# Retention with two gated layers: where queries are decayed, who copies the outputs, and in which order scores are made

## The chip, the cores and the metric

The kernel runs on one core of a Trainium2 chip. The metric is the device time of one launch in microseconds (us), the median of several runs. The core has five engines that work side by side, each in the order of its own queue: TensorE (PE, with its weight loads as PEld), VectorE (DVE), ScalarE (ACT), GpSimd (POOL) and SyncE (SP), which here issues the DMAs.

## The reference, cut to what matters

```python
scores = q @ k^T / sqrt(64)                    # B=4, H=8, S=576, head size 64
Dmat   = gamma_h ** (i - j) for i >= j, else 0 # gamma_h = 1 - 2**(-5-h)
ret    = (scores * Dmat) @ v                   # retention, no softmax
x = ret as (2304, 512)
x = (h * tanh(softplus(h))) @ w_out,  h = x @ w_in      # first layer, "mish", 512 -> 2048 -> 512
out = (h * sigmoid(1.702 h)) @ w2_out, h = x @ w2_in    # second layer
```

## The kernel before, in words

**Retention.** A batch of 576 tokens is cut into five chunks, four of 128 tokens and a last one of 64; batch by batch they make 20 units, u = 0 to 19. The unit's tile `unit` (1 MB; `rest`, 512 KB, for the short ones, units 4, 9, 14 and 19) holds q and k transposed, and v and k by token. The decay gamma^(i-j) is split into a factor for the query, in the table `gt`, and one for the value, in `vt`, so that only a causal mask `cm` is left for the scores. Each unit takes these steps:

- `decay_v(u)`: POOL multiplies v by `vt` in place (line 866).
- `scores(u)`: PE makes k^T q for 8 heads (`sc`, line 875), DVE masks them into two tiles `pm` (line 879).
- `update(u)` and `take(u)`: PE adds k^T v to the running sums `ds` (line 898), ACT copies them to `state` (line 133, two instructions). Short units have neither.
- `outputs(u)`: PE adds the earlier state times q (line 926; not in the first unit of a batch) and v times `pm` (line 938) in a bank `o`.
- `finish(u)`: the rows of `o` are multiplied by `gt` and put into X (line 956, DVE).

The loop over u writes these out by hand; each engine follows the order in which they are written. In step u stand `decay_v(u + 1)`, then POOL's share of other jobs, then `scores(u + 1)`, `update(u)`, `take(u)`, `outputs(u)`, ACT's early jobs, `finish(u)`, DVE's jobs, ACT's late jobs, and in eight units a piece of `split_x` (ACT, then DVE line 403), which splits X into a high and a low part for the first layer.

**The other jobs** are the conversions of the first layer's weights, one of which starts every unit or so, in pieces that `position(name, step)` hands out: DVE clamps (line 202), ACT scales (line 133, two instructions), DVE masks and shifts (lines 142 and 214), POOL joins (line 218), ACT rounds to the high part, DVE subtracts to get the low part (line 250). Weights 0 start in units 8 and 9, weights 1 in units 13 and 14, weights 2 in unit 18.

**The layers.** The first product of the first layer (`up`, line 416) already starts in steps 17 and 18, between the last units; then PE goes through 32 slots of the first layer, and through the rest of the program.

The banks are fixed: scores rotate over banks 0 to 3 (two per unit), `o` over 6 and 7, `ds` over 4 and 5.

Of the kernel before, what the change touches and what calls it, by code (L numbers as in the profile page):

```python
# [8 lines left out]
F32 = mybir.dt.float32  # L9
# [4 lines left out]
AF = mybir.ActivationFunctionType  # L14
ALU = mybir.AluOpType
# [5 lines left out]
P = 128  # L21
NPAIR = H // 2
# [3 lines left out]
CH = [(c, min(P, S - c)) for c in range(0, S, P)]  # L26
NCH = len(CH)
UNITS = [(b, c) for b in range(B) for c in range(NCH)]
# [31 lines left out]
REST = CH[-1][1]  # L60
SPLIT = 5
LAST = 2 * NPAIR * REST + DM

# [35 lines left out]
def retention_mish_gelu_kernel(ctx: ExitStack, tc: tile.TileContext, qkv, w1, w2, first_unit, rests, out):  # L101
    nc = tc.nc
    keep = ctx.enter_context(tc.tile_pool(name="keep", bufs=1))
# [4 lines left out]
    def cut(k, o, n):  # L108

        s, o = divmod(o, 2 * TH)  # L110
        assert o + n <= 2 * TH
        return X[:, s, k, o : o + n]
# [12 lines left out]
    def bank(kind, of):  # L125
        taken[kind] = taken.get(kind, -1) + 1
        return ps.tile([P, NB], F32, tag=f"b{of[taken[kind] % len(of)]}", name=kind)

    def quarters(t):
        return t.rearrange("p (c n) -> p c n", c=NPAIR)  # L130

    def act(o, i, f=AF.Copy, scale=1.0, bias=0.0):
        nc.scalar.activation(out=o, in_=i, func=f, scale=scale, bias=bias)  # L133
# [22 lines left out]
    def position(name, step):  # L156
        for j in [j for j in under_way if j[1] == name]:
            j[1] = next(j[0], None)
            if j[1] is None:
                under_way.remove(j)  # L160
        while plans.get(name) and plans[name][0][0] <= step:
            job = plans[name].pop(0)[1]
            then = next(job, None)
            if then:
                under_way.append([job, then])
# [197 lines left out]
    n_u = len(UNITS)  # L363
# [22 lines left out]


    xs, hs, gs, acc, side = {}, {}, {}, {}, []

    column = keep.tile([P, 32], F32, name="column")  # L390

    def split_x(t, k):

# [402 lines left out]
    def attention():  # L796
        with tc.tile_pool(name="att", bufs=1) as ap:
            loaded = {}
# [10 lines left out]
            def load(u):  # L809

                b, c = UNITS[u]
                if c == NCH - 1:
                    t = ap.tile([P, LAST], F32, tag="rest", name="rest", bufs=2)
                    nc.sync.dma_start(out=t, in_=rests[b])
                    loaded[u] = views(t, REST)
                    return
                t = buffers[(u - b) % len(buffers)]
                if u == 0:
                    for e0, e in ((0, 2 * DM), (2 * DM, FIRST)):
                        nc.sync.dma_start(out=t[:, e0:e], in_=first_unit[:, e0:e])  # L820
                else:
                    for e in (0, 2 * DM) if u == 1 else (0,):
                        e1 = e + 2 * DM if u == 1 else 4 * DM
                        nc.sync.dma_start(out=t[:, e:e1], in_=qkv[b, c, :, e:e1])
                loaded[u] = views(t, P)

            state = [ap.tile([P, NPAIR, P], F32, name=f"state{i}") for i in range(2)]
# [17 lines left out]
                out=cm, in_=cm, pattern=[[1, P]], compare_op=ALU.is_ge, fill=0.0, base=0, channel_multiplier=-1  # L845
            )
            gt = ap.tile([P, NCH, NPAIR, P], F32, name="gt")
# [3 lines left out]
            for _ in range(WARM):  # L851
                nc.tensor.matmul(unused, lhsT=zeros, rhs=zeros, start=True, stop=True)

            act(column[:, :1], state[0][:, 0, :1], AF.Mish)

            for u in range(1, NCH + 1):
                load(u)
            pm, sums, now = {}, [None], [None]

            def decay_v(u):  # L860
                b, c = UNITS[u]
                n = CH[c][1]
                vv = loaded[u][2][:n].rearrange("p (h d) -> p h d", d=D)
                for eng, h, e in ((nc.vector, 0, SPLIT), (nc.gpsimd, SPLIT, H)) if u == 0 else ((nc.gpsimd, 0, H),):
                    by = vt[:n, c, h:e].unsqueeze(2).to_broadcast([n, e - h, D])
                    eng.tensor_tensor(out=vv[:, h:e], in0=vv[:, h:e], in1=by, op=ALU.mult)

            def scores(u):
                n = CH[UNITS[u][1]][1]
                qt, kt = loaded[u][:2]  # L870
                sc = [quarters(bank("sc", (0, 1, 2, 3))) for _ in range(2)]
                for p in range(NPAIR):
                    for j in range(2):
                        sl = slice(64 * j, 64 * j + 64)
                        nc.tensor.matmul(sc[j][:n, p, :n], lhsT=kt[sl, p, :], rhs=qt[sl, p, :], start=True, stop=True)  # L875
                pm[u] = []
                for j in range(2):
                    t = ap.tile([P, NPAIR, P], F32, tag="pm", name="pm", bufs=4)
                    nc.vector.tensor_tensor(
                        out=t[:n, :, :n],  # L880
                        in0=sc[j][:n, :, :n],
                        in1=cm[:n, :n].unsqueeze(1).to_broadcast([n, NPAIR, n]),
                        op=ALU.mult,
                    )
                    pm[u].append(t)

            def update(u):

                c = UNITS[u][1]
                if c == NCH - 1:  # L890
                    return
                v, kk = loaded[u][2:]
                if c == 0:
                    sums[0] = quarters(bank("ds", (4, 5)))
                for p in range(NPAIR):
                    for j in range(2):
                        sl = slice(p * P + 64 * j, p * P + 64 * j + 64)
                        nc.tensor.matmul(  # L898
                            sums[0][64 * j : 64 * j + 64, p, :D],
                            lhsT=kk[:, sl],  # L900
                            rhs=v[:, sl],
                            start=(c == 0 and p == 0),
                            stop=True,
                            skip_group_check=True,
                        )
# [43 lines left out]
            def finish(u, o):  # L949
                b, c = UNITS[u]  # L950
                t0, n = CH[c]
                g0 = b * S + t0
                part = 0
                while part < n:
                    w = min(n - part, 2 * TH - (g0 + part) % (2 * TH))
                    nc.vector.tensor_tensor(
                        out=cut(slice(None), g0 + part, w),
                        in0=o[:, :, part : part + w],
                        in1=gt[:, c, :, part : part + w],
                        op=ALU.mult,  # L960
                    )
                    part += w

            decay_v(0)
# [5 lines left out]
            for u in range(n_u):  # L970
                step = u - n_u
                if u - 1 in wide and wide.index(u - 1) + len(buffers) < len(wide):
                    n = wide[wide.index(u - 1) + len(buffers)]
                    load(n)
                    if n + 1 not in wide:
                        load(n + 1)
                if u + 1 < n_u:
                    decay_v(u + 1)
                position("pool", step)
                position("fetch", step)  # L980
                if u == 0:
                    for n in wide[NCH : len(buffers)]:
                        load(n)
                if NCH - 1 <= u < n_u - 1:
                    scores(u + 1)
                before = now[0]

                def step_state():
                    update(u)
                    now[0] = take(u)  # L990

                if u != 1:
                    step_state()
                o = outputs(u, before, *((step_state,) if u == 1 else ()))
                if 0 < u < NCH - 1:
                    scores(u + 1)
                if u < NCH - 1:
                    n = CH[u + 1][1]
                    for p in range(NPAIR):
                        act(gt[:, u + 1, p, :n], gt[:, 0, p, :n], scale=steps[:, p, u + 1 : u + 2])  # L1000
                position("act early", step)

                if u == n_u - 2:
                    elementwise(0, jobs=False)
                finish(u, o)
                if u == n_u - 1:
                    elementwise(1, jobs=False)
                if u == 0:
                    scores(1)
                position("vector", step)  # L1010
                position("act late", step)
                if u in X_UNITS:
                    k = X_UNITS.index(u)
                    split_x((0, SIDE)[k // NK], k % NK)()
                if u == n_u - 3:
                    up(0)
                if u == n_u - 2:
                    up(1)
# [266 lines left out]
```

## Time and profile before

| | before |
|---|---|
| median of 3 runs (lowest, highest) | 807.36 us (807.34, 808.15) |
| the profiled execution's own time | 807.84 us |
| its span, first to last instruction | 806.1 us |
| PE busy | 801.2 us (99%) |
| DVE, ACT, POOL busy | 571.2, 442.0, 189.3 us |
| mean granted TensorE clock | 0.999 |
| retention, from the first score to the last output | about 5 to 70 us |

The span is what the trace shows; the 1.7 us between it and the execution's time lie before the first and after the last instruction. A busy PE says only that a matmul was under way; whether it was held up is read from the distance of the starts in the timeline.

### The profile page before, as it was taken

Reading aid. Unit: us, or ns where it says so; the run is one execution under the profiler, and the core shown is the slowest. Engines: PE = TensorE matmul, PEld = TensorE weight load, DVE = VectorE, ACT = ScalarE, POOL = GpSimd, SP = SyncE. Lnnn points to the kernel's source line nnn. Section 1 sums busy time; section 2 is a strip of 40 time slices with the busy share of each in tenths; the row PEclk is TensorE's granted clock in tenths of the full one; section 3 lists DMA queues with packets and bytes.
Section 4 is the critical chain, followed back from the end, with each engine's and each line's share of the span. In section 5 each row is a group of like instructions: output and inputs, shape, how many; then the busy total and the mean of one; then the engine's idle time right before and its main releaser. Section 6 shows DMA issues by size and latency. Waiting matters only on the chain.

```text
span 806.1 us, 14287 instructions
## 1 busy us (share of the span) xinstructions
PE 801.2 (99%) x5394; PEld 761.7 (94%) x5394; DVE 571.2 (71%) x992; ACT 442.0 (55%) x861; POOL 189.3 (23%) x251
## 2 busy tenths in 40 slices
PE   9999999999999999999999999999999999999998
PEld 8998888889999999999999999999999999999998
DVE  3897988877687676567677376798555897656775
ACT  5355867765766565666566454665233663234542
POOL 3352322220376460366570052000000000000000
PEclk9999999999999999999999999999999999999999
DMA  9994679746799895698986599888887888878884
GB/s 363 420 375 123 231 235 287 273 143 214 275 309 327 297 336 177 204 324 310 341 289 219 200 351 382 272 275 270 291 255 253 252 272 291 272 253 257 251 272 158
DMA packets 92325, 219.68 MB, mean 273 GB/s; under 512 B 6496, under 2 KB 52576, under 8 KB 90464
## 3 DMA queue, kind: packets, MB, share of 16 engines
q1 hardware_dynamic: 92112, 218.56, 80.4%
q8 instruction: 43, 0.70, 0.3%
q14 instruction: 26, 0.21, 0.1%
q10 hardware_dynamic: 144, 0.20, 0.1%
HBM read 169.98 MB, written 48.76 MB: 271 GB/s over the span
## 4 chain that ended last, share of the span: by engine, by line
PE 97%; DVE 1%; DMA 1%; ACT 0%; POOL 0%; issue 0%; SPq 0%
PE p L731 22%; PE p L682 21%; PE acc L1093 17%; PE p L1156 15%; PE h L416 8%; PE acc L437 8%; PE sc L875 2%; PE o L938 2%; PE o L926 2%; PE ds L898 1%; DMA unit<-first_unit_dram 1%; DVE cs L475 0%; DVE u L475 0%; DVE X L142 0%; ACT cs L133 0%; DVE cy L352 0%
## 5 line engine op out<-in xcount | busy, mean ns | idle before, releaser
L682 PE MATMUL p<-xop,ring 128*128 128x384 f32 x1008 | 175.6, 334 | 0.4 <-DVE cs L475 0.4
L682 PEld LDWEIGHTS p<-xop,ring 128*128 128x128 f32 x1008 | 174.7, 188 | 0.8 <-DVE cs L475 0.7
L731 PE MATMUL p<-g,ring 128*128 128x384 f32 x1008 | 175.2, 334 | 0.0
L731 PEld LDWEIGHTS p<-g,ring 128*128 128x128 f32 x1008 | 174.8, 188 | 0.0
L1093 PE MATMUL acc<-g,w 128*128 128x512 f32 (+1 forms) x768 | 143.7, 337 | 0.0
L1093 PEld LDWEIGHTS acc<-g,w 128*128 128x128 f32 x768 | 124.3, 188 | 17.1 <-DVE g L475 0.2
L1156 PE MATMUL p<-xop,ring 128*128 128x384 f32 x672 | 128.4, 337 | 0.0
L1156 PEld LDWEIGHTS p<-xop,ring 128*128 128x128 f32 x672 | 115.7, 188 | 0.3
L133 ACT ACTIVATE g<-cs 128x384 fp32r<-128x384 f32 x168 | 79.0, 517 | 60.3 <-PE p L731 60.0
L475 DVE TENSOR_TENSOR g<-cs,g 128x384 fp32r<-128x384 f32 x168 | 90.0, 554 | 26.7 <-ACT g L133 25.0
L133 ACT ACTIVATE cs<-cs 128x384 f32<-128x384 f32 x72 | 37.8, 526 | 104.7 <-DVE cs L475 104.7
L437 PE MATMUL acc<-g,w 128*128 128x512 f32 (+1 forms) x384 | 72.3, 337 | 0.0
L475 DVE TENSOR_TENSOR g<-c,g 128x384 fp32r<-128x384 f32 x64 | 44.4, 693 | 38.9 <-ACT g L133 38.5
L437 PEld LDWEIGHTS acc<-g,w 128*128 128x128 f32 x384 | 60.2, 190 | 7.6
L133 ACT ACTIVATE c<-p 128x384 f32<-128x384 f32 x64 | 31.2, 488 | 52.7 <-PE p L1156 52.5
L218 POOL TENSOR_TENSOR raw<-raw 128x512 int32<-128x512 int32 x32 | 36.5, 1141 | 96.3 <-DVE raw L214 87.0
L342 POOL TENSOR_TENSOR cy<-cy 128x128 f32<-128x128 f32 x88 | 54.3, 626 | 5.2
L475 DVE TENSOR_TENSOR cs<-cs 128x384 f32<-128x384 f32 x96 | 53.4, 556 | 0.8
L416 PE MATMUL h<-x,w 128*128 128x512 f32 x192 | 46.4, 390 | 0.0
L218 POOL TENSOR_TENSOR cy<-cr 128x256 int32<-128x256 int32 x38 | 31.2, 842 | 62.7 <-DVE cr L214 58.3
L133 ACT ACTIVATE raw<-raw 128x512 int32<-128x512 uint32 x64 | 40.6, 679 | 7.8 <-DVE raw L202 7.5
L475 DVE TENSOR_TENSOR c<-p,c 128x384 f32<-128x384 f32 x48 | 26.5, 553 | 23.9 <-ACT c L133 12.9
(94 smaller groups left out, 971.6 us busy)
## 6 DMA issues: line engine op xcount, KB each, us to landing
ring<-stream SPq DMA_DIRECT2D x168, 512.0 KB, 4.6
ring<-first_stream SPq DMA_DIRECT2D x56, 512.0 KB, 5.5
stream<-cy SPq DMA_DIRECT2D x22, 896.0 KB, 5.0
raw<-w_dram SPq DMA_DIRECT2D x32, 512.0 KB, 8.0
unit<-qkv_dram SPq DMA_DIRECT2D x14, 1024.0 KB, 13.4
cr<-w_dram SPq DMA_DIRECT2D x19, 512.0 KB, 5.7
stream<-X SPq DMA_DIRECT2D x10, 896.0 KB, 5.4
first_stream<-cy SPq DMA_DIRECT2D x16, 512.0 KB, 3.0
```

What stands on the lines that cost most here:

```text
L133: nc.scalar.activation(out=o, in_=i, func=f, scale=scale, bias=bias)
L218: nc.gpsimd.tensor_tensor(out=o, in0=upper, in1=bits, op=ALU.add)
L342: nc.gpsimd.tensor_tensor(out=v[:, o], in0=v[:, a], in1=v[:, b], op=op)
L416: nc.tensor.matmul(h[:, :n], lhsT=W[0, m // 2][:, m % 2, a, k * P : (k + 1) * P], rhs=xs[t, k][:, b, :n], start=((k, a, b) == order[0]), s ...
L437: nc.tensor.matmul(acc[t, e][:, :n], lhsT=W[1, m // 2][:, m % 2, a, e * P : (e + 1) * P], rhs=g[:, b, :n],  start=(begins(i) and a == 0 an ...
L475: eng.tensor_tensor(out=o, in0=a, in1=b, op=op)
L682: nc.tensor.matmul(banks[p], lhsT=w[:, k, a * P : (a + 1) * P], rhs=x[:, b, k], start=(p not in SAME and k == 0 and a == 0 and b == 0), st ...
L731: nc.tensor.matmul(banks[e, p], lhsT=w[:, e, a * P : (a + 1) * P], rhs=g[:, b], start=(p != 2 and r == 0 and a == 0 and b == 0), stop=(r = ...
L875: nc.tensor.matmul(sc[j][:n, p, :n], lhsT=kt[sl, p, :], rhs=qt[sl, p, :], start=True, stop=True)
L926: nc.tensor.matmul(o[sl, p, :n], lhsT=before[:, p, sl], rhs=qt[:, p, :], start=(p == 0), stop=True, skip_group_check=True,)
L1093: nc.tensor.matmul(acc[t, e][:, :w], lhsT=W[1, m // 2][:, m % 2, a, e * P : (e + 1) * P], rhs=g[:, b, o : o + w], start=(m == 0 and a == 0 ...
L1156: nc.tensor.matmul(bank, lhsT=w[:, a, k * P : (k + 1) * P], rhs=x[:, b, k], start=(p in (1, 2, 7) and k == 0 and a == 0 and b == 0), stop= ...
```

## The change

From unit 6 on (`SCALED`), the decay of the query is applied to q instead of to the output: a new `decay_q(u)` on POOL multiplies the query part of the unit's tile by `gt` in place, two steps ahead (three for units 11 to 19) of the step in which the unit's outputs are made, and `finish(u)` is a plain copy on ACT. From unit 12 on (`TWICE`), the scores of two units are made one after the other in every second step. `pm` gets six buffers instead of four, and a scratch column is dropped (its one use writes into `gt`, ahead of the table).

```diff
+SCALED = 6
+TWICE = 12
...
-    column = keep.tile([P, 32], F32, name="column")
...
-            act(column[:, :1], state[0][:, 0, :1], AF.Mish)
+            act(gt[:, 0, 0, :1], state[0][:, 0, :1], AF.Mish)
...
+            def decay_q(u):
+                c = UNITS[u][1]
+                n = CH[c][1]
+                nc.gpsimd.tensor_tensor(out=loaded[u][0], in0=loaded[u][0], in1=gt[:, c, :, :n], op=ALU.mult)
...
-                    t = ap.tile([P, NPAIR, P], F32, tag="pm", name="pm", bufs=4)
+                    t = ap.tile([P, NPAIR, P], F32, tag="pm", name="pm", bufs=6)
...
-                    nc.vector.tensor_tensor(
-                        out=cut(slice(None), g0 + part, w),
-                        in0=o[:, :, part : part + w],
-                        in1=gt[:, c, :, part : part + w],
-                        op=ALU.mult,
-                    )
+                    to, of = cut(slice(None), g0 + part, w), o[:, :, part : part + w]
+                    if u >= SCALED:
+                        act(to, of)
+                    else:
+                        nc.vector.tensor_tensor(out=to, in0=of, in1=gt[:, c, :, part : part + w], op=ALU.mult)
...
+                for n in range(SCALED, n_u):
+                    if u == n - 2 - (n > TWICE - 2):
+                        decay_q(n)
                 position("pool", step)
...
-                    scores(u + 1)
+                    for n in (u + 1,) if u + 1 < TWICE else (u + 1, u + 2) if (u + 1 - TWICE) % 2 == 0 else ():
+                        scores(n)
```

**PE, from the scores of unit 12 to those of unit 15, before.** `sc` are scores, `ds` the sums, `o` the outputs (from `state`, then from `pm`).

```order
L875 MATMUL sc<-unit 128x128 x8
L898 MATMUL ds<-unit 64x64 x8
L926 MATMUL o<-unit,state_72 64x128 x8
L938 MATMUL o<-pm,unit 64x128 x8
L875 MATMUL sc<-unit 128x128 x8
L898 MATMUL ds<-unit 64x64 x8
L926 MATMUL o<-unit,state_73 64x128 x8
L938 MATMUL o<-pm,unit 64x128 x8
L875 MATMUL sc<-rest 64x64 x8
```

PE at the same place, from the scores of units 12 and 13 on, in the changed kernel (its lines are numbered a little higher: 880 is 875, 903 is 898, 931 is 926, 943 is 938):

```order
L880 MATMUL sc<-unit 128x128 x16
L903 MATMUL ds<-unit 64x64 x8
L931 MATMUL o<-unit,state_71 64x128 x8
L943 MATMUL o<-pm,unit 64x128 x8
L903 MATMUL ds<-unit 64x64 x8
L931 MATMUL o<-unit,state_72 64x128 x8
L943 MATMUL o<-pm,unit 64x128 x8
L880 MATMUL sc<-rest 64x64 x8
L880 MATMUL sc<-unit_75 128x128 x8
```

The scores of unit 13 moved up beside those of unit 12, ahead of the sums and outputs of unit 11; those of unit 15 stand right behind those of unit 14.

**POOL, from v of unit 11 to v of unit 15, before.** Line 866 is `decay_v`, line 218 a weight's join.

```order
L866 TENSOR_TENSOR unit<-unit,unit_76 128x512
L218 TENSOR_TENSOR raw<-raw 128x512
L866 TENSOR_TENSOR unit<-unit,unit_76 128x512
L218 TENSOR_TENSOR raw<-raw 128x512
L866 TENSOR_TENSOR unit<-unit,unit_76 128x512
L866 TENSOR_TENSOR rest<-rest,unit_76 64x512
L866 TENSOR_TENSOR unit_76<-unit_76 128x512
```

POOL at the same place in the changed kernel, from v of unit 11 on; line 871 is `decay_q`, here for units 13, 14, 15, 16 and 17, and line 220 the join:

```order
L866 TENSOR_TENSOR unit<-unit,unit_75 128x512
L871 TENSOR_TENSOR unit<-unit,gt 128x512
L220 TENSOR_TENSOR raw<-raw 128x512
L866 TENSOR_TENSOR unit<-unit,unit_75 128x512
L871 TENSOR_TENSOR rest<-rest,gt 128x256
L220 TENSOR_TENSOR raw<-raw 128x512
L866 TENSOR_TENSOR unit<-unit,unit_75 128x512
L871 TENSOR_TENSOR unit_75<-unit_75,gt 128x512
L866 TENSOR_TENSOR rest<-rest,unit_75 64x512
L871 TENSOR_TENSOR unit_76<-unit_76,gt 128x512
L866 TENSOR_TENSOR unit_75<-unit_75 128x512
L871 TENSOR_TENSOR unit_77<-unit_77,gt 128x512
```

Between two operations on v there is now one on q, and the one on q is that of a unit two further on.

**DVE in steps 10 to 13, before**: masks (line 879), outputs (line 956), the first layer's operands (line 403) and weights (lines 142, 214, 250).

```order
L142 SCALAR_TENSOR_TENSOR raw<-raw 128x512
L214 TENSOR_SCALAR raw<-raw 128x512
L403 TENSOR_TENSOR side<-X,side 128x256
L879 TENSOR_TENSOR pm<-sc,cm 128x512 x2
L956 TENSOR_TENSOR X<-o,gt 128x4x128
L250 TENSOR_TENSOR w_622<-raw,w_622 128x512
L403 TENSOR_TENSOR side<-X,side 128x256
L879 TENSOR_TENSOR pm<-sc,cm 128x512 x2
L956 TENSOR_TENSOR X<-o,gt 128x4x128
L250 TENSOR_TENSOR w_673<-raw,w_673 128x512
L403 TENSOR_TENSOR side<-X,side 128x256
L879 TENSOR_TENSOR pm<-sc,cm 64x4x64 x2
```

DVE at the same place in the changed kernel; line 144 is 142, 216 is 214, 252 is 250, 884 is 879:

```order
L144 SCALAR_TENSOR_TENSOR raw<-raw 128x512
L216 TENSOR_SCALAR raw<-raw 128x512
L403 TENSOR_TENSOR side<-X,side 128x256
L884 TENSOR_TENSOR pm<-sc,cm 128x512 x4
L252 TENSOR_TENSOR w_629<-raw,w_629 128x512
L403 TENSOR_TENSOR side<-X,side 128x256
L252 TENSOR_TENSOR w_695<-raw,w_695 128x512
L403 TENSOR_TENSOR side<-X,side 128x256
L884 TENSOR_TENSOR pm<-sc,cm 64x4x64 x2
L884 TENSOR_TENSOR pm<-sc,cm 128x512 x2
```

The outputs are gone; the masks of units 12 and 13 stand together, and four operations on weights and operands stand in a row ahead of the mask of unit 14.

## Rows read from the trace of the kernel before

**Rows 1.** Page, chain that ended last: share of the span by engine

```profile
PE 97%; DVE 1%; DMA 1%; ACT 0%; POOL 0%; issue 0%; SPq 0%
```

**Rows 2.** Waits of PE, 0 to 170 us: us in total, times, longest

```profile
PE o L938 <- DVE pm L879: 0.2, 1, 0.2
```

**Rows 3.** Timeline of PE, units 11 to 15: start, duration, instructions

```profile
40.23 1.16 PE L875 MATMUL sc<-unit 64*128 64x128 f32 x16
41.33 0.69 PE L898 MATMUL ds<-unit 128*64 128x64 f32 x16
41.84 1.04 PE L926 MATMUL o<-unit,state 128*64 128x128 f32 x16
42.72 1.04 PE L938 MATMUL o<-pm,unit 128*64 128x128 f32 x16
43.69 1.16 PE L875 MATMUL sc<-unit 64*128 64x128 f32 x16
...
46.17 1.04 PE L938 MATMUL o<-pm,unit 128*64 128x128 f32 x16
47.15 0.68 PE L875 MATMUL sc<-rest 64*64 64x64 f32 x16
47.76 0.69 PE L898 MATMUL ds<-unit 128*64 128x64 f32 x16
...
51.83 0.68 PE L938 MATMUL o<-pm,rest 64*64 64x64 f32 x16
52.44 1.16 PE L875 MATMUL sc<-unit 64*128 64x128 f32 x16
53.53 0.69 PE L898 MATMUL ds<-unit 128*64 128x64 f32 x16
```

**Rows 4.** Groups by line and shape, 20 to 62 us: busy us, mean ns

```profile
L956 DVE TENSOR_TENSOR X<-o,gt 128x512 f32<-128x512 f32 x10 | 6.8, 682 | 1.5 <-PE o L938 1.5
L956 DVE TENSOR_TENSOR X<-o,gt 128x256 f32<-128x256 f32 x5 | 2.0, 414 | 0.9 <-PE o L938 0.9
L214 DVE TENSOR_SCALAR raw<-raw 128x512 int32<-128x512 int32 x4 | 1.7, 430 | 0.1
```

**Rows 5.** Groups of ACT by shape, 190 to 260 us

```profile
L133 ACT ACTIVATE X<-acc 128x512 f32<-128x512 f32 x2 | 1.2, 595 | 0.4 <-PE acc L437 0.4
```

**Rows 6.** Timeline of POOL, 32 to 48 us

```profile
32.85 1.04 POOL L866 TENSOR_TENSOR unit<-unit,unit 128x512 f32<-128x512 f32 x1 [3.98 <-DMA unit<-qkv_dram]
35.28 1.04 POOL L866 TENSOR_TENSOR unit<-unit,unit 128x512 f32<-128x512 f32 x1 [1.39 <-DMA unit<-qkv_dram]
...
43.98 1.04 POOL L866 TENSOR_TENSOR unit<-unit,unit 128x512 f32<-128x512 f32 x1
44.98 1.48 POOL L866 TENSOR_TENSOR rest<-rest,unit 64x512 f32<-64x512 f32 x1
46.43 1.04 POOL L866 TENSOR_TENSOR unit<-unit 128x512 f32<-128x512 f32 x1
```

**Rows 7.** Timeline of DVE, 44 to 51 us

```profile
44.83 0.73 DVE L250 TENSOR_TENSOR w<-raw,w 128x512 fp32r<-128x512 f32 x1
45.49 2.26 DVE L403 TENSOR_TENSOR side<-X,side 128x256 fp32r<-128x256 f32 x1
47.67 1.28 DVE L879 TENSOR_TENSOR pm<-sc,cm 128x512 f32<-128x512 f32 x2
...
50.35 0.41 DVE L403 TENSOR_TENSOR side<-X,side 128x256 fp32r<-128x256 f32 x1
50.69 0.74 DVE L879 TENSOR_TENSOR pm<-sc,cm 64x256 f32<-64x256 f32 x2
```

**Rows 8.** Timeline of ACT: the state of unit 15

```profile
54.32 0.78 ACT L133 ACTIVATE state<-ds 64x256 f32<-64x256 f32 x2 [1.25 <-PE ds L898]
```

**Rows 9.** Timeline of DVE: the low part of weights 2 of the first layer

```profile
77.16 0.68 DVE L250 TENSOR_TENSOR w<-raw,w 128x512 fp32r<-128x512 f32 x1
```

**Rows 10.** Timeline of PE: the product that takes weights 2

```profile
77.74 1.52 PE L416 MATMUL h<-x,w 128*128 128x512 f32 x6
```

## Prediction

> **What bounds it.** I first read the chain that ended last: PE holds 97% of the span [rows 1]. Then PE's waits over the retention and the first layer: a single one, of 0.2 us [rows 2]. So while the retention runs, PE is never kept waiting by the engines that the change relieves, and nothing taken from DVE or given to ACT or POOL is a gain by itself. What can be won is PE's own time, and for that the timeline's starts count, not its durations, since matmuls overlap. From one start to the next, the outputs from the state take 0.88 us (41.84 to 42.72), those from the masked scores 0.97 (42.72 to 43.69), the scores 1.09 (43.69 to 44.78), the sums 0.51 (41.33 to 41.84) [rows 3]. Outputs and scores are the same number of matmuls with the same 128 moving columns; what the scores have more, and what the outputs have more when scores follow, is the price of changing from tiles of 128 by 64 to 64 by 128 and back.
>
> **What the pairs save on PE.** Outputs before scores cost 0.97 - 0.88 = 0.09 more, scores 1.09 - 0.88 = 0.21 more, and sums behind scores 0.51 where half of 0.88, for half the columns, would be 0.44: 0.07 more. A round trip is thus 0.37 us with four places where it is paid, of which some belongs to the wider weights of the scores; I take 0.17 for one change of tiles. By the order, PE changes tiles 22 times from unit 12's scores to the first layer before, and 17 times after: the pairs 12 and 13, 16 and 17 save two changes each; 14 and 15, 18 and 19 pair a short unit's 64 by 64 tiles with a long one's and save less; the sums behind the product in step 17 cost one more kind of change and one less. Five times 0.17 is **-0.85 us**. Bounds: 0 (the extra belongs to the scores themselves) and -1.0.
>
> **What moves between the engines.** DVE loses ten wide and five narrow copies, 6.8 + 2.0 = 8.8 us [rows 4]. ACT gains them; the nearest row is its copy of 512 elements from a bank, 0.595 us [rows 5], so at most 15 x 0.6 = 9 us, hidden behind PE: a bank `o` is used again only two units on, some 3.5 us a unit later. POOL gains 14 multiplications. The nearest row is its multiplication of v at 1.04 us [rows 6]; for a short unit's 256 elements I take half, bounds 0.5 and 1.04. That is 11 x 1.04 + 3 x 0.5, some 13 us, in a stretch in which POOL sat idle for 1.4 to 4 us between units. For units 6 to 12 this idle time covers them. The dropped column and the two more buffers cost nothing: the write goes to the same engine that fills the table later, and the buffers remove a wait that PE does not have.
>
> **Where it does not fit.** In steps 10 to 14 POOL has 11 operations in a row (v and q of five units, two joins), and DVE has eight operations that touch POOL's port. What that costs stands in the rows: the weight subtraction at 44.83, 0.68 us alone [rows 9], found POOL busy from 43.98 to 45.02 and ended 0.54 us behind it; POOL's next multiplication then took 1.48 us where it takes 1.04, ending 0.90 us behind DVE's end. The narrow subtraction at 45.49, 0.41 us alone, took 2.26 us and ended at 47.75, 0.28 us behind the second of two POOL operations [rows 6, 7]. Masks read a bank, and keep their 0.64 us. So I let the two alternate: a DVE operation ends 0.28 us (narrow, clamp, shift) or 0.54 us (wide) after the POOL operation ahead of it, the next POOL operation 0.90 us after that. In the Trainium skill, SBUF — State Buffer, section "SBUF: two separate sides", DVE and POOL share a port pair as an exclusive lock, and whichever starts first holds it for its whole instruction. By that rule each wait lasts one operation, as in my sum; the row at 45.49 shows two, which is the rival below.
>
> Now the walk, in the clock of the rows before, against the times at which PE would come without waits.
> - Unit 13's q. Loads land 2.43 us apart (35.28 - 32.85 [rows 6], units 10 and 11, both waiting for them), so unit 13's lands near 40.1 (estimate). Then it takes its turn with a shift on DVE and ends near 41.3. PE wants it right behind unit 12's scores, at 40.23 + 0.99 = 41.22: **0.1 us**. (Before, at 43.69.)
> - Masks of unit 12. Ahead of them on DVE stand a clamp (ends 41.6), unit 11's masks (to 42.8), then line 142, which finds POOL at v of unit 12 (to 43.5; ends 44.05), the shift behind q of unit 14 (44.5; ends 44.8), and the narrow subtraction, which takes the port at once (45.15). Masks to 46.35. PE wants them at 46.17 - 0.34 = 45.83, with the wait above 45.95: **0.4 us**.
> - Unit 15's q. POOL goes on with the join (45.15 + 0.90 = 46.05), v of unit 13 (47.05), q of unit 15 (48.1). PE: unit 14's scores at 47.15 - 0.35, 0.61 for them, so 47.41, now 47.95: **0.1 us** more.
> - Masks of unit 14. Unit 13's are done at 47.55. Then two wide and two narrow subtractions, and POOL busy throughout with q 15, v 14, q 16, v 15: they end at 48.6, 49.8, 51.25 and 52.45, the mask (0.74 [rows 7]) at 53.1. PE wants it for `o` of unit 14 at 51.83 - 0.55 = 51.28, now 51.9: **1.1 us**. If nothing waited, the masks would be ready at 50.1; that is the lower bound, 0.
> - Unit 16's sums go into the bank from which ACT copies unit 15's state. That copy ended at 54.32 + 0.78 = 55.10 [rows 8], 1.57 us behind the start of the sums at 53.53. With no scores between, PE is there after 0.52 + 0.88 = 1.40: **0.2 us**.
>
> Behind these waits stand all of PE's later matmuls, since its queue is in order; nothing gives the time back, as PE is the chain. Later pairs have room: POOL's q 17 is ready a unit ahead. Sum: -0.85 + 0.1 + 0.4 + 0.1 + 1.1 + 0.2 = **+1.05 us**. The profiled execution took 807.84 us, 0.48 above the median, so against the median 807.36 this gives **808.4 us**.
>
> **The first layer** sets a cap on gains. The low part of weights 2 is ready at 77.16 + 0.68 = 77.84 [rows 9], and PE's product that needs it, from its third matmul on, begins at 77.74 [rows 10], some 0.45 us ahead of that matmul: 0.35 us to spare. DVE no longer has the last two outputs ahead of it, but ACT now waits there for unit 19's output before it can go on, so that chain comes perhaps 0.2 us earlier, not 0.85. A retention shorter by more than 0.55 us is not passed on in full. With the loss that I forecast this does not bind.
>
> **Rivals.**
> - The port costs little (DVE slips in between, or POOL is never so far behind): no more than the 0.1 and 0.2 us of the first and last item. The gain is then -0.85 + 0.3 = -0.55, just at the cap: 806.8 us. For it: the masks have 1.8 us of room if nothing waits, and DVE is 8.8 us lighter. Against: 11 POOL operations in a row, and rows 7.
> - DVE loses the port again and again, as at 45.49: each loss adds one POOL operation, 1.04 us, ahead of a mask that PE waits for. Two of them on the way to the masks of units 12 and 14 give 808.4 + 2.1 = 810.5 us. It is slower by over 0.2% from a sum of waits of 2.5 us on. For it: that row; against: in the same place DVE got the port after one operation.
> - The pairs save nothing, because the 0.21 us belongs to the scores' own wide weight loads: 807.36 + 1.9 = 809.3 us. For it: no row shows two wide scores in a row; against: the outputs ahead of the scores, with no wide weights, take 0.09 longer too.
>
> **How the numbers follow.** A change of 0.2%, 1.6 us, is about what a measurement of this kernel can tell from none. Forecast (807.7 to 809.0 us): 0.44. Cheap port (806.5 to 807.7): 0.27. Port lost repeatedly: 0.20. No saving: 0.05. Faster by more than 0.2% has no mechanism here, since PE's saving ends at 1.0 us; 0.04 is for what I overlook. Slower by over 0.2% is the third and fourth case and the edge of the first: 0.26; the same: 0.70. The range reaches from the cheap port's 806.6 us into the repeated losses, to 810.2.
>
> **What would show it.** After: the second scores of a pair follow the first after 1.0 us, not 1.09, and one pair saves 0.35 us. PE's waits should name POOL's q for the scores of units 13 and 15, DVE's masks for the outputs of units 12 and 14, and ACT's state for the sums of unit 16. DVE's subtractions at line 252 and 403 should take 1 us and more. I am wrong if PE still waits for nothing (then it is faster, by up to 0.55 us), or if waits come in units 6 to 11, which I took to be covered.

## The result: slower by 1.1%

The changed kernel took 816.56 us (median of 4 runs, 815.53 to 816.72) beside 807.64 us for the kernel before: a ratio of 1.0107, interval 1.0090 to 1.0125. The prediction of 808.4 us and its range up to 810.2 were wrong. Its profiled execution took 816.72 us with a span of 815.0 us, 8.9 us more than before; the mean clock was 0.996.

The chain that ended last, share of the span by engine, after, answers to [rows 1]:

```profile
PE 95%; DVE 3%; DMA 1%; issue 0%; ACT 0%; POOL 0%; SPq 0%
```

PE's share fell by two hundredths and DVE's rose by two. The waits of PE after (us in total, times, longest) say where; before, there was a single one of 0.2 us [rows 2], which is still there (at 7.56 us) as the shorter of the two for masks:

```profile
PE o L943 <- DVE pm L884: 4.7, 2, 4.5
PE sc L880 <- POOL unit L871: 1.0, 2, 0.8
```

The timeline of PE after (start, duration, instructions), from the scores of units 12 and 13 to the sums of unit 18, answers to [rows 3]:

```profile
40.14 1.16 PE L880 MATMUL sc<-unit 64*128 64x128 f32 x16
42.11 1.22 PE L880 MATMUL sc<-unit 64*128 64x128 f32 x16 [0.81 <-POOL unit L871]
43.26 0.69 PE L903 MATMUL ds<-unit 128*64 128x64 f32 x16
...
47.94 0.68 PE L880 MATMUL sc<-rest 64*64 64x64 f32 x16
48.85 1.16 PE L880 MATMUL sc<-unit 64*128 64x128 f32 x16 [0.23 <-POOL unit L871]
...
52.21 0.64 PE L931 MATMUL o<-rest,state 128*64 128x64 f32 x16
57.32 1.35 PE L943 MATMUL o<-pm,rest 64*64 64x64 f32 x16 [4.48 <-DVE pm L884]
58.61 3.78 PE L880 MATMUL sc<-unit 64*128 64x128 f32 x32
...
64.61 0.63 PE L903 MATMUL ds<-unit 128*64 128x64 f32 x16
...
73.95 0.69 PE L903 MATMUL ds<-unit 128*64 128x64 f32 x16
```

Two things are to be seen: the outputs of unit 14 from its masks come at 57.32, 5.1 us behind the outputs from the state; and behind them the scores of units 16 and 17 take 3.7 us until the next instruction, where the scores of two units otherwise take 2. What DVE and POOL did in those 5 us is in their timelines. Below, q 15 is short for POOL's multiplication of unit 15's queries (line 871), v 15 for that of its values (line 866). DVE, which answers to [rows 7]:

```profile
45.59 2.47 DVE L884 TENSOR_TENSOR pm<-sc,cm 128x512 f32<-128x512 f32 x4
47.98 1.36 DVE L252 TENSOR_TENSOR w<-raw,w 128x512 fp32r<-128x512 f32 x1
49.27 2.49 DVE L403 TENSOR_TENSOR side<-X,side 128x256 fp32r<-128x256 f32 x1
51.68 2.76 DVE L252 TENSOR_TENSOR w<-raw,w 128x512 fp32r<-128x512 f32 x1
54.37 2.48 DVE L403 TENSOR_TENSOR side<-X,side 128x256 fp32r<-128x256 f32 x1
56.77 1.93 DVE L884 TENSOR_TENSOR pm<-sc,cm 64x256 f32<-64x256 f32 x4
```

POOL, which answers to [rows 6]:

```profile
47.53 1.27 POOL L871 TENSOR_TENSOR unit<-unit,gt 128x512 f32<-128x512 f32 x1
48.76 1.49 POOL L866 TENSOR_TENSOR rest<-rest,unit 64x512 f32<-64x512 f32 x1
50.21 1.27 POOL L871 TENSOR_TENSOR unit<-unit,gt 128x512 f32<-128x512 f32 x1
51.44 1.22 POOL L866 TENSOR_TENSOR unit<-unit 128x512 f32<-128x512 f32 x1
52.63 1.27 POOL L871 TENSOR_TENSOR unit<-unit,gt 128x512 f32<-128x512 f32 x1
53.86 1.48 POOL L866 TENSOR_TENSOR unit<-unit,unit 128x512 f32<-128x512 f32 x1
55.31 1.25 POOL L871 TENSOR_TENSOR unit<-unit,gt 128x512 f32<-128x512 f32 x1
```

The four subtractions, 0.68 and 0.41 us alone, took 1.36, 2.49, 2.76 and 2.48. Lay their ends beside POOL's: the first ended at 49.34, 0.54 behind the multiplication of q 15 (48.80); the second at 51.76, 0.28 behind q 16 (51.48); the third at 54.44, 0.54 behind q 17 (53.90); the fourth at 56.85, 0.29 behind q 18 (56.56). The first waited for one operation of POOL, each of the others for two: the rest of one on v that was already under way, and the whole of the one on q behind it.

The windows of after (engines busy with their instructions, then PEclk, DMA share, GB/s) explain the second thing:

```profile
50.00:57.00 7.00, 2.84 (x66) 2.70 (x64) 7.00 (x4) 2.21 (x5) 6.56 (x6) 1.00 1.00 404
57.00:64.00 7.00, 6.68 (x72) 6.29 (x74) 6.27 (x13) 1.37 (x4) 2.83 (x3) 0.53 0.25 99
64.00:71.00 7.00, 7.00 (x141) 6.47 (x137) 4.71 (x8) 5.45 (x11) 4.04 (x3) 0.98 0.01 2
```

After the wait the granted clock was near its lower level, 1.2 GHz, and it was back at the upper one from 64.6 us on. With the waits and the clock, the account of the loss can be closed once there is a kernel with the same matmuls in the same order and without them. That is the first experiment.

### The profile page after: what moved, and what is told of

It is laid out like the page before. It is cut to its first block, busy times and chain, and to the rows that moved or that the text cites. A ratio compares the mean times of both kernels' runs of the same rounds, so it can differ in the third digit from the quotient of the medians.

```text
span 815.0 us, 14290 instructions
## 1 busy us (share of the span) xinstructions
PE 804.5 (99%) x5394; PEld 764.7 (94%) x5394; DVE 571.9 (70%) x977; ACT 448.6 (55%) x876; POOL 208.2 (26%) x265
## 4 chain that ended last, share of the span: by engine, by line
PE 95%; DVE 3%; DMA 1%; issue 0%; ACT 0%; POOL 0%; SPq 0%
PE p L731 21%; PE p L682 20%; PE acc L1101 16%; PE p L1164 14%; PE h L416 8%; PE acc L437 8%; PE sc L880 2%; PE o L943 2%; PE o L931 1%; PE ds L903 1%; DVE pm L884 1%; DMA unit<-first_unit_dram 1%; DVE side L403 1%; DVE w L252 0%; DVE cs L475 0%
## 5 line engine op out<-in xcount | busy, mean ns | idle before, releaser
L416 PE MATMUL h<-x,w 128*128 128x512 f32 x192 | 46.7, 392 | 0.0
L416 PEld LDWEIGHTS h<-x,w 128*128 128x128 f32 x192 | 35.7, 188 | 8.2 <-DVE g L457 0.4
```

Of the source, the lines that this page charges most:

```text
L416: nc.tensor.matmul(h[:, :n], lhsT=W[0, m // 2][:, m % 2, a, k * P : (k + 1) * P], rhs=xs[t, k][:, b, :n], start=((k, a, b) == order[0]), s ...
```

## Experiments

The theory after reading the trace: POOL's added multiplications keep the port that it shares with DVE busy, DVE's four subtractions lose it for two operations at a time, PE waits for unit 14's masks, and its clock falls on top. The rivals: the order in pairs makes the wait by itself; ScalarE's copies do; or the subtractions are slow for a reason of their own.

**Pairs alone.** Nothing is scaled on POOL; outputs are multiplied by DVE.

```diff
-SCALED = 6
+SCALED = 20
```

> The pairs of scores alone: the query is not scaled on GpSimd, the outputs are scaled by VectorE as before. Port theory (VectorE's subtractions wait for the GpSimd operations that were added): without those operations the mask of unit 14 is ready near 50.8 us, ahead of TensorE, no wait over 0.3 us, the clock stays full, and the 0.85 us of tile changes are saved, at most 0.55 of it passed on: 806.8 to 807.4 us, ratio 0.999 to 1.000. Order theory (the mask of unit 14 is late because the pairs move four operations ahead of it, whoever is on the port): a wait of 2 us or more at the outputs of unit 14 stays, and the time is 811 us or more.

Measured: 807.49 us, ratio 1.0001 (0.9992 to 1.0010). PE's timeline in this run:

```profile
40.21 2.06 PE L880 MATMUL sc<-unit 64*128 64x128 f32 x32
42.20 0.69 PE L903 MATMUL ds<-unit 128*64 128x64 f32 x16
...
46.77 0.68 PE L880 MATMUL sc<-rest 64*64 64x64 f32 x16
47.38 1.16 PE L880 MATMUL sc<-unit 64*128 64x128 f32 x16
...
51.67 0.68 PE L943 MATMUL o<-pm,rest 64*64 64x64 f32 x16
...
55.98 0.69 PE L903 MATMUL ds<-unit 128*64 128x64 f32 x16 [0.15 <-ACT state L135]
...
65.36 0.69 PE L903 MATMUL ds<-unit 128*64 128x64 f32 x16
```

The pairs alone don't make the loss. They do save: from unit 12's scores to unit 14's it is 46.77 - 40.21 = 6.56 us, before 47.15 - 40.23 = 6.92 [rows 3]. That the time stays the same is because the gain is spent again: at unit 16's sums, which wait for unit 15's state, and between unit 15's scores and unit 14's outputs from its masks, which takes 4.29 us here and 3.92 in the quarter of the scaling below. There the profile lists no wait, and why it is longer is not shown.

From start to start, the same stretches in the two kernels (us):

| stretch | pairs alone | after | more |
|---|---|---|---|
| scores 12 to sums 11 | 1.99 | 3.12 | 1.13 |
| to scores 14 | 4.57 | 4.68 | 0.11 |
| to scores 15 | 0.61 | 0.91 | 0.30 |
| to outputs of unit 14 from its masks | 4.29 | 8.47 | 4.18 |
| to sums of unit 16 | 4.31 | 7.29 | 2.98 |
| to sums of unit 18 | 9.38 | 9.34 | -0.04 |

Together 8.66 us, less 0.07 by which the changed kernel came earlier to unit 12's scores: 8.59, which is 73.95 - 65.36.

**Scaling alone.** The scores stay one unit a step.

```diff
-TWICE = 12
+TWICE = 20
```

> The scaling on GpSimd and the copies on ScalarE alone, scores unit by unit as before. Port theory: VectorE's subtractions at lines 252 and 403 still take 2 us and more in steps 11 to 13, since the same GpSimd operations stand beside them; TensorE waits for a mask, but with two and not four such operations ahead of each mask by less: 1 to 3 us of waits, 808.5 to 812 us. Order theory: no wait of TensorE, 807.6 us, the subtractions as short as before.

Measured: 811.65 us, ratio 1.0051 (1.0038 to 1.0065). PE waits 1.0 us for unit 14's masks, 0.4 for POOL's queries, 0.4 for ACT's copies; one subtraction of line 403 took 2.49 us here too. These listed waits are only a part: by its starts PE comes to unit 18's sums 3.3 us later than before (68.81 beside 65.49). So the scaling loses by itself, and the pairs, which put the four subtractions in a row ahead of a mask, more than double it.

**A quarter of the scaling.** Each multiplication of queries takes one of four head pairs; three quarters of the scaling are left out. The instructions, their order and their waits stay.

```diff
-                nc.gpsimd.tensor_tensor(out=loaded[u][0], in0=loaded[u][0], in1=gt[:, c, :, :n], op=ALU.mult)
+                nc.gpsimd.tensor_tensor(out=loaded[u][0][:, :1], in0=loaded[u][0][:, :1], in1=gt[:, c, :1, :n], op=ALU.mult)
```

> The changed kernel, but GpSimd scales one of four head pairs only (a quarter of the work is left out, the other pairs stay unscaled): as many GpSimd operations in the same order, each of some 0.5 us in place of 1.27. Port theory (a VectorE operation waits for whole GpSimd operations): VectorE's subtractions end within 1.5 us, the mask of unit 14 comes before TensorE wants it or within 0.3 us of it, 806.8 to 807.8 us. Order theory: the wait of 4.5 us at the outputs of unit 14 and the fallen clock stay, 814 us or more.

Measured: 807.83 us, ratio 1.0004 (0.9995 to 1.0013). The wait for unit 14's masks is gone, with ScalarE's copies still in place, which clears them of it. It is POOL's time that counts, not the number of its operations.

**Splits later.** The pieces of `split_x`, whose subtractions were two of the four, go to units 14 to 17.

```diff
-X_UNITS = (4, 5, 6, 7, 10, 11, 12, 13)
+X_UNITS = (4, 5, 6, 7, 14, 15, 16, 17)
```

> The changed kernel, with the four narrow subtractions of line 403 moved from steps 10 to 13 to steps 14 to 17. Port theory: two operations in place of four stand ahead of the mask of unit 14, it comes 5 us earlier and TensorE does not wait for it (0.3 us at most); the moved ones wait in later steps, in front of masks that are wanted later: 807 to 809 us. If the mask is late for a reason other than VectorE's row of subtractions, the wait of 4.5 us stays and the time with it, 816 us.

Measured: 811.33 us, ratio 1.0048 (1.0035 to 1.0062). The long wait is gone, but the time is above what was expected: PE waits 2.1 us at scores, put down to POOL's queries: 0.8 at unit 6's (23.22 us; q 6 was done at 23.17, in the changed kernel at 22.55, ahead of the scores at 22.77) and 1.3 at unit 13's. That part of the expectation was wrong; the last experiment comes back to unit 13.

**The wait filled.** 18 matmuls on zeros into a bank of their own, between the two halves of unit 14's outputs; they add nothing to the result.

```diff
+FILL = 18
...
+                if u == 14:
+                    filler = ps.tile([P, NB], F32, tag="b4", name="filler")[:, :P]
+                    for _ in range(FILL):
+                        nc.tensor.matmul(filler, lhsT=zeros, rhs=zeros, start=True, stop=True)
```

> The changed kernel with 18 more matmuls on zeros (some 4.2 us at full clock), into a free bank, between the two halves of unit 14's outputs, where TensorE waits 4.5 us for the mask. Clock theory (TensorE's clock falls to its lower level because of that wait, and the 7.3 us that the next steps then take, against 4.3 us in the run with a quarter of the scaling, are its price): the granted clock stays at its upper level behind the wait, the mask comes at the same time, and 3 us come back: 813.0 to 814.0 us. If the slow steps have another cause (banks, the port), they stay slow and the time is 816.5 us or more.

Measured: 814.23 us, ratio 1.0085 (1.0072 to 1.0099), 2.3 us less than the changed kernel, for more work, and 0.2 above the range expected. (The outputs from the masks start behind the filling, at 57.67 us, 0.35 later than in the changed kernel.) The window of after's slow stretch, in this run:

```profile
57.00:64.00 7.00, 6.84 (x132) 6.33 (x132) 6.56 (x14) 3.81 (x8) 2.85 (x3) 1.00 0.27 105
```

The clock stays at its upper level, and from unit 14's outputs to unit 16's sums it is 4.31 us, as with the pairs alone. So the 2.98 us of the table is the clock, and the clock fell because PE stood.

**Three pairs.** The pairs alone, with units 16 and 17 in single steps, so that nothing waits for unit 15's state (`SCALED = 20`, and):

```diff
-                    for n in (u + 1,) if u + 1 < TWICE else (u + 1, u + 2) if (u + 1 - TWICE) % 2 == 0 else ():
+                    for n in (u + 1,) if u + 1 < TWICE or u + 1 in (16, 17) else (u + 1, u + 2) if (u + 1 - TWICE) % 2 == 0 else ():
```

> The pairs alone, without the scaling, and units 16 and 17 one by one: that pair saves 0.35 us and gives 0.33 us back, since the sums of unit 16 wait for the state of unit 15. Expected: no such wait, some 0.1 to 0.4 us less than with all pairs, 806.9 to 807.4 us; a ratio to the kernel before between 0.9990 and 1.0005, which 5 rounds can hardly tell from 1.

Measured: 807.30 us, ratio 0.9997 (0.9988 to 1.0006): not to be told from before. The wait for the state is gone, but so are two changes of tiles saved.

**The end as before.** The quarter of the scaling, and units 18 and 19 neither scaled nor copied by ScalarE.

```diff
-                    if u >= SCALED:
+                    if SCALED <= u < 18:
...
-                for n in range(SCALED, n_u):
+                for n in range(SCALED, 18):
```

> A quarter of the scaling as above (the rest of it is left out, and units 18 and 19 are not scaled on GpSimd at all), and units 18 and 19 leave their banks by VectorE as before. If it is ScalarE's copies of units 18 and 19 that make the first layer's weights 2 late, TensorE's product with them starts its third matmul without a wait, the low part is ready 0.3 us or more ahead of it, and the span is 0.4 us shorter than with a quarter of the scaling: 805.7 us. Otherwise the weights are ready 0.06 us ahead of it again, which is a wait, and the span stays at 806.1 us.

Measured: 807.49 us in one run, span 805.8 beside 806.1 for the quarter of the scaling. The first layer's product that takes weights 2 lasts 2.88 us, as in the trace of before, and 3.15 with ScalarE's copies. In the changed kernel too that product is held up; the low part on DVE, and the product on PE:

```profile
86.16 0.68 DVE L252 TENSOR_TENSOR w<-raw,w 128x512 fp32r<-128x512 f32 x1
```

```profile
86.30 3.17 PE L416 MATMUL h<-x,w 128*128 128x512 f32 x12
```

DVE starts 0.14 us ahead of PE, where before it was 0.58 [rows 9, 10]. The products ahead of and behind this one show the cost. After:

```profile
83.44 2.91 PE L437 MATMUL acc<-g,w 128*128 128x512 f32 x12
89.31 1.60 PE L437 MATMUL acc<-g,w 128*128 128x256 f32 x12
```

With the pairs alone:

```profile
74.85 2.91 PE L437 MATMUL acc<-g,w 128*128 128x512 f32 x12
80.32 1.59 PE L437 MATMUL acc<-g,w 128*128 128x256 f32 x12
```

From start to start that is 5.87 us beside 5.47: 0.40 us of the loss lie here. With the 8.59 us of the table that makes the 9.0 by which the changed kernel's span is longer than that of the pairs alone (815.0 and 806.0 us).

**Another kind of subtraction.** The same values by `scalar_tensor_tensor`, at lines 252 (shown) and 403.

```diff
-        nc.vector.tensor_tensor(out=lo, in0=value, in1=hi.bitcast(F32), op=ALU.subtract)
+        stt(lo, value, 1.0, hi.bitcast(F32), ALU.mult, ALU.subtract)
```

> The changed kernel with VectorE's subtractions at lines 252 and 403 written as a three-operand instruction (value times 1, minus high part), the kind that line 144 has, which waited for one GpSimd operation each time. If the kind of instruction decides whether VectorE waits for one GpSimd operation or two: at most 1.6 us for each, mask of unit 14 near 53 us, a wait of TensorE of 1 to 1.5 us and no fall of the clock, 808.5 to 810 us. If the place decides (a subtraction right behind another, GpSimd's queue full): 2.5 us for three of the four as before, 816 us.

Measured: 816.51 us, ratio 1.0110 (1.0097 to 1.0124), with the four durations 1.37, 2.49, 2.76 and 2.48 again. The kind of instruction doesn't decide. Nor does the kind at line 144 always wait for one operation, as the expectation has it: with the splits later it took 1.94 us at 55.61, through the rest of v 16 and the whole of q 18. With scaling alone a clamp at line 204, 0.41 us alone, took 1.82.

**Units 6 to 15 scaled.** The multiplications of q 16, q 17 and q 18 are gone from the stretch of the four subtractions.

```diff
-                    if u >= SCALED:
+                    if SCALED <= u < 16:
...
-                for n in range(SCALED, n_u):
+                for n in range(SCALED, 16):
```

> Both parts of the change, but only units 6 to 15 are scaled on GpSimd; units 16 to 19 are multiplied by VectorE when they are copied out, as before. This takes the multiplications of the queries of units 16, 17 and 18 out of the stretch of 50 to 57 us, where VectorE's four subtractions stand ahead of unit 14's masks. If what delays them is that GpSimd always has a next operation to take the port with, the first two subtractions still wait, GpSimd runs dry behind the values of unit 16 (near 52.5 us), the last two take 0.4 to 1.3 us, and TensorE's wait for unit 14's masks falls from 4.6 to 1 to 2 us, without the fall of the clock: 810 to 812 us. If the four subtractions are slow for a reason of their own place (data that comes late, their own writes), they stay at 2.5 us and the time stays at 815 to 817 us. Unit 13's wait for its queries (1.0 us, near 42 us) stays in both.

Measured: 810.03 us, ratio 1.0034 (1.0021 to 1.0047). The subtractions took 1.36, 0.52, 1.53 and 1.26 us, and PE has no wait for unit 14's masks at all. So q 16 to q 18 were the second operations for which DVE had waited. The time is as expected by another way: unit 6's scores waited 0.5 us and unit 13's 1.4. Behind the latter the clock fell in the profiled execution, which this account had not foreseen:

```profile
44.50:46.70 2.20, 2.20 (x33) 2.20 (x34) 2.17 (x5) 0.76 (x2) 1.83 (x3) 0.60 1.01 421
46.70:48.40 1.70, 1.70 (x21) 1.70 (x20) 1.70 (x4) 0.00 (x0) 1.70 (x2) 0.51 1.05 429
```

That execution took 811.33 us at a mean clock of 0.998. The other four took 809.89 to 810.08 us at 1.000, so the median holds no fall of this size.

**Units 16 to 19 scaled.** The other way round (`SCALED = 16`): q 16 to q 18 stay, but POOL has no backlog when they come.

> Both parts of the change, but only units 16 to 19 are scaled on GpSimd and copied by ScalarE. The queries of units 13 to 15 are then not multiplied, so the scores of unit 13 wait for nothing, and GpSimd is not behind when the four subtractions begin; only the queries of units 16 to 18 come between the values of units 15, 16 and 17, which GpSimd does as the loads land, 2.4 us apart. By the port theory a subtraction meets at most two operations on end now and then and waits 0.7 to 2 us; the masks of unit 14 have 1.8 us of room, so TensorE waits 0 to 0.8 us for them: 807.2 to 808.8 us. If the multiplication of the queries of units 16 to 18 alone makes the loss, the wait stays above 2 us and the time above 810 us.

Measured: 808.74 us, ratio 1.0014 (1.0005 to 1.0024). No wait for unit 14's masks; the longest that is left is at unit 17's scores, 0.7 us, for POOL's queries. The four subtractions ran at 0.42 to 0.68 us, as they came ahead of q 16. The backlog without these three multiplications did not make the long wait, nor did the three without the backlog; together they did.

**Masks between.** The two masks of unit 13 stand behind the first and the second subtraction, so that the second and third no longer stand right behind another one.

```diff
+                if u == TWICE + 1:
+                    masks.extend((mask, j) for j in range(2))
+                else:
+                    mask(0)
+                    mask(1)
...
                 position("vector", step)
+                next_mask()
...
                     split_x((0, SIDE)[k // NK], k % NK)()
+                next_mask()
```

> The whole change; only the two masks of unit 13 are placed otherwise on VectorE: one behind the first of the four subtractions, one behind the second, so that the second and third subtraction each stand behind a mask, which does not use the port, and only the fourth stands right behind another subtraction. If a subtraction loses the port twice because it stands right behind another one, the second and third take about one GpSimd operation less each (1.3 instead of 2.5 us), the wait for unit 14's masks falls from 4.6 to some 2 us, and the time to 811 to 814 us, by whether the clock still falls. If the loss depends on GpSimd's full queue alone and not on what stands ahead on VectorE, they stay at 2.2 to 2.8 us, and the time stays at 815.5 to 817.5 us.

Measured: 811.78 us, ratio 1.0055 (1.0040 to 1.0070): 4.8 us less than the changed kernel, by moving two masks. PE's wait for unit 14's masks is 0.9 us, and the clock stays at 1.00. DVE in this run:

```profile
41.83 1.27 DVE L892 TENSOR_TENSOR pm<-sc,cm 128x512 f32<-128x512 f32 x2
...
48.53 0.90 DVE L403 TENSOR_TENSOR side<-X,side 128x256 fp32r<-128x256 f32 x1
49.35 0.68 DVE L892 TENSOR_TENSOR pm<-sc,cm 128x512 f32<-128x512 f32 x1
49.95 2.15 DVE L252 TENSOR_TENSOR w<-raw,w 128x512 fp32r<-128x512 f32 x1
52.03 2.50 DVE L403 TENSOR_TENSOR side<-X,side 128x256 fp32r<-128x256 f32 x1
```

The second subtraction gained as expected (0.90 for 2.49), the third hardly (2.15, behind a mask), so the idea that a subtraction loses because it stands right behind another holds in part only. A POOL that never pauses isn't enough either: with units 6 to 15 scaled it went on from v 14 to v 15 to v 16 (48.88, 50.33, 51.51 us), and DVE waited for one operation each time. When DVE loses the port for a second operation stays open.

This run also corrects the reading of one wait. The scores of unit 13 came here at 42.60, put down to POOL; but POOL's multiplication of q 13 was done at 41.62:

```profile
40.17 1.45 POOL L871 TENSOR_TENSOR unit<-unit,gt 128x512 f32<-128x512 f32 x1
```

```profile
42.60 1.71 PE L887 MATMUL sc<-unit 64*128 64x128 f32 x16 [1.44 <-POOL unit L871]
```

What ended just ahead is the first of unit 11's two masks, near 42.51 (41.83 and the 0.68 of one mask). Scores rotate over four banks, two a unit, so unit 13's go into unit 11's, one bank for each mask. With the splits later, the wait filled and units 6 to 15 scaled the same distance, 0.09 or 0.10 us, stands between the first mask and unit 13's scores. The sums of unit 11, next on PE, start 1.14 us behind the end of the second mask in these four runs and in the quarter of the scaling, and 1.15 in the changed kernel (42.11 and 43.26):

```profile
40.84 1.27 DVE L884 TENSOR_TENSOR pm<-sc,cm 128x512 f32<-128x512 f32 x2
```

There q 13 ended at 42.06, within 0.05 us of the second mask, so which of the two held unit 13's scores cannot be told; the masks were late because the clamp ahead of them, 0.41 us alone, took 1.27 behind v 12. This is read from times; no run of its own tests it.

## Why the prediction was wrong

**The step that failed** is the one on the masks of unit 14: 1.1 us, from the rule that a DVE operation waits for one POOL operation and that the two alternate. The wait was 4.5 us, since three of the four subtractions waited for two. In the walk they took 1.05, 1.2, 1.45 and 1.2 us; on the chip 1.36, 2.49, 2.76 and 2.48. The delay behind POOL's end was right within 0.01 us (0.28 narrow, 0.54 wide); the count was not, and the row at 45.49 [rows 7] had shown two. I made the one row that lost a rival at 0.20 and the neighbour that won the rule, on one row each. In the Trainium skill, SBUF — State Buffer, section "SBUF: two separate sides", whichever of the two starts first holds the shared pair for the whole instruction; the trace agrees as to the whole instruction, and says that a DVE operation that already waits may still see POOL's next one go first, three times in a row here.

**The rival that DVE loses again and again** had the right mechanism and sign, with two losses of 1.04 us on the way to the masks of units 12 and 14. There were three, all ahead of unit 14's masks, and a multiplication of q took 1.27 us, not the 1.04 of one of v, from which its duration was taken.

**A term was missing:** the clock, 2.98 us. I had the price of every wait as its own length; this wait of 4.5 us cost 2.98 more. With unit 14's masks (4.18 by the table), unit 13's scores (1.13), weights 2 (0.40) and unit 15's q (0.30) this names nearly all of the 9.0 us against the pairs alone.

**Unit 13's q:** 0.1 forecast. The stretch with it took 1.13 us longer (table), 0.97 of it ahead of the scores (they start 1.97 behind unit 12's, due after 1.0). The cause named, q 13, ended at 42.06, and unit 11's masks, which free the banks, at 42.11; either would have made nearly the whole of it. My walk let unit 11's masks end at 42.8 and yet had unit 13's scores at 41.3 in the same banks: a wait that its own numbers held and that I did not see.

**The smaller terms:** masks of unit 12, 0.4 forecast; by the table the outputs of unit 12 were 0.11 late at most, since PE was already late from unit 13's scores. Unit 15's q: 0.1 forecast, 0.30 by the table. Unit 16's sums behind unit 15's state: 0.2 forecast and 0.2 listed in the pairs alone and in the quarter of the scaling. Units 6 to 12, which I took to be covered, had no wait of their own in the changed kernel's trace, but q 6 held up unit 6's scores by 0.8 and 0.5 us in two of the runs.

**The saving of the pairs** held where it can be read alone: 0.36 us for one pair beside 0.35 forecast, and two sets of scores in 1.99 us, where one takes 1.09. As a whole it was mis-sized: with the pairs alone PE goes from unit 12's scores to the first product at line 437 in 34.64 us (40.21 to 74.85), before in 34.76 (40.23 to 74.99), 0.12 less, where 0.85 less the 0.2 of unit 16's sums was forecast. **The cap** I said would not bind with a loss did bind, by 0.4 us: ScalarE's copies came ahead of its work on weights 2, whatever the retention took.

## What to carry to other kernels

An idle engine is not free to take work if it shares a port with one whose results are waited for: price the move by the operations that then stand ahead of each deadline, and count two operations of the other engine per wait until the trace shows one. Reckon a stall of TensorE that is longer than any the kernel had at more than its length, by the granted clock behind it. And when an operation is moved ahead in its engine's order, ask when its output buffers come free, not only when its inputs are ready.

## What was not expected of the hardware

- A DVE operation of 0.41 us took 2.49 us, through the rest of one GpSimd operation and the whole of the next (1.27 us); three operations in a row fared so (2.49, 2.76, 2.48), and in the same way with another kind of instruction.
- A GpSimd multiplication of 128 x 512 took 1.27 us for q with its table, and 1.04 for v with a factor spread over each head [rows 6].
- The granted clock was 0.53 from 57 to 64 us, behind a wait of 4.5 us. With units 6 to 15 scaled it fell behind a wait of 1.4 us (0.51 at 46.7 to 48.4) in one execution of five, by their mean clocks; with the masks between it did not, behind one of 1.44 us. What tells these apart stays open.
